# Key heads computed in spare weight columns and gathered by DMA, and value products taken in pairs, in a one-core attention and feed-forward kernel

## The chip, the cores and the metric

The kernel runs on one core of one Trainium2 chip. The metric is the device time of one execution in microseconds (us). Each kernel was run several times, on the same chip as the kernel that it is compared with and in the same rounds. The profiler's span of an execution is some 1.7 us shorter than its device time; times inside a profile count from the start of the span.

## The reference, cut to what matters

The sequence has 2048 positions of width 448. Sixteen heads of 28 columns attend to 8 keys, 2 positions apart. The attention output gates a feed-forward branch of width 1792.

```python
xn = layernorm(x)                                   # (1, 2048, 448)
qkv = (xn @ wqkv).reshape(B, S, 3, 16, 28)...       # q, k, v
idx = pos[:, None] - 2 * arange(8)[None, :]         # 8 keys, distance 2
logits = einsum("bhsd,bhswd->bhsw", q, k[idx]) * 28 ** -0.5   # masked where idx < 0
s = (softmax(logits) @ v[idx]) @ wo
g = silu(gelu(xn @ w1 + b1) @ w2 + b2)
return x + s * g
```

## The kernel before

Positions are split by parity, so that a distance of 2 becomes a distance of 1. There are four chunks of 512 positions and 17 attention units of 121 queries. A stage is the first feed-forward product of one chunk, then the q and k projections of the next chunk, then (in the first three stages) five attention units, each beside one tile of the second feed-forward product. I call the stages first, second and last by the five units that they hold (0 to 4, 5 to 9, 10 to 14). Within a stage I number the units from 0.

The 448 rows of contraction are three times 128 and a rest of 64. Two rests share the array: one uses its upper 64 rows, the other its lower 64 rows. I call such a product half-height. Heads lie four to a group, each in a slot of 32 columns of which 28 are the head's.

```python
    def qk_weights(which, kt):
        r = slice(0, P) if kt < 3 else slice(64 * which, 64 * which + 64)
        src = wraw[r, kt, D * which:D * which + 32]
        nc.vector.tensor_copy(wqk[r, kt, H * which:H * which + H, :],
                              bass.AP(src.tensor, src.offset, [list(src.ap[0]), [DH, H], [1, 32]]))

    def qk_full(c, g, ps, first, copies):          # six products, 128 rows of contraction
        for w in range(2):                         # w = 0: q, w = 1: k
            for kt in range(3):
                nc.tensor.matmul(ps[w][:, :], wqk[:, kt, 16 * w + 4 * g:16 * w + 4 * g + 4, :],
                                 xnT[:, kt, LEAD + c * CH:LEAD + (c + 1) * CH], ...)
            ...
    # qk_rest: the two half-height products; qk_pair(c, g): both, for head group g of chunk c

    def qk_put(c, g, w, ps, copies):
        copies[w]((qT, kT)[w][:, g, LEAD + c * CH:LEAD + (c + 1) * CH], ps[w][:, :])

    def v_mm(b):                                   # value product of block b: four products
        ps = psB.tile([P, D], F32, name="ps_v", tag="B")
        o = LEAD + QB * b - 7
        for kt in range(KT):
            nc.tensor.matmul(ps[:, :], xnT[:, kt, o:o + P], wv[:, kt, :], ...)
        return ps
    ...
        # one stage
        feed_forward_1(c, ps, ...)                 # holds qk_pair(c + 1, 0)
        qk_pair(n, 1, True, DD)                    # n = c + 1
        for i in range(5):
            b = next(units)
            if i == 0:
                E = qk_unit(b, lambda: qk_pair(n, 2, False, ...))   # scores S, exp, mask
                ...
                qk_pair(n, 3, True, DA)
            else:
                E = qk_unit(b)
                norm()
                ffn2_job(4 * c + i - 1)            # y
                v_job(next(vs))
                if n + 1 < NC:
                    ln_apply(4 * n + 3 + i)
                    ln_dma(4 * n + 3 + i)          # SyncE: transpose into xnT
            norm = av_unit(b, E)                   # O, attention times values
```

Nearly every transfer is issued from SyncE, in program order: the loads of weights and x at the start, `late_loads()` (the last 512 rows of x and 16 pieces of `wo`) after the first four transposes, the transposes of normalised x, and the stores of finished output tiles `o_t`, of which there are three buffers.

The softmax here doesn't subtract the row's maximum and nothing guards it: scores larger than these inputs give would overflow.

## Time and profile before

| | before |
|---|---|
| median of the first three runs | 167.68 us (167.32 to 167.9) |
| profiled span | 165.6 us |
| TensorE (PE) busy | 158.9 us, 96% |
| its longest wait after the start | under 0.4 us |

These are two lines of the timeline of SyncE's queue (start in us, length of the group in us, line, operation, destination and source, count).

```profile
27.30 8.16 SPq L140 DMA_DIRECT2D wo<-in_A_wo_dram  x16
...
41.65 13.69 SPq L184 DMA_TRANSPOSE xnT<-xnb  x4
```

The reader is to see that the queue issues one transfer after another, that sixteen small ones took 8.16 us of it, and that it was then free from 35.46 to 41.65, before the transposes that the second stage's projections need.

### The profile page before, as it was taken

The page shows a single profiled execution, that of the slowest core. Times are in us where ns is not written, and L with a number is a line of the kernel's source. Part 1 is how long each engine was busy: PE and PEld are TensorE (multiplying, and loading weights), DVE is VectorE, ACT ScalarE, POOL GpSimd, SP SyncE. Part 2 cuts the span into 40 slices and gives each one's busy share as a digit, 9 for nine tenths or more (in the row PEclk, how much of TensorE's full clock was granted, in tenths as well). Part 3 has the DMA queues.
Part 4 walks back from the last instruction along what each step waited for, and adds up shares of the span by engine and source line. Part 5 has one row for each costly group of instructions (what it writes and reads, how often), then busy time and mean ns, then how long its engine had stood idle before and what let it go on. Part 6 is the DMA issues. An engine that isn't in the chain of part 4 may idle for free.

```text
span 165.6 us, 3242 instructions
## 1 busy us (share of the span) xinstructions
PE 158.9 (96%) x1290; PEld 71.8 (43%) x1301; DVE 112.9 (68%) x256; ACT 125.9 (76%) x198; POOL 4.5 (3%) x16
## 2 busy tenths in 40 slices
PE   6899999999999999999999999999999999999990
PEld 2343333345554334445554334335555334445570
DVE  5967890497888638687888308877777507678893
ACT  3773698598887795998887795698888698698830
POOL 7002000000000000000000000000000000000000
PEclk9999999999999999999999999999999999999999
DMA  5999995520111100100211100300000002020011
GB/s 134 302 306 267 325 190 93 164 44 4 32 36 32 32 0 4 55 0 0 36 32 32 36 0 0 112 1 4 0 4 0 0 0 60 31 83 0 4 55 55
DMA packets 15963, 10.62 MB, mean 64 GB/s; under 512 B 7500, under 2 KB 15948, under 8 KB 15948
## 3 DMA queue, kind: packets, MB, share of 16 engines
q1 hardware_dynamic: 15660, 10.18, 24.0%
q10 hardware_dynamic: 288, 0.23, 0.5%
q8 instruction: 10, 0.16, 0.4%
q14 instruction: 5, 0.04, 0.1%
HBM read 7.00 MB, written 1.84 MB: 53 GB/s over the span
## 4 chain that ended last, share of the span: by engine, by line
PE 83%; ACT 7%; DVE 5%; DMA 2%; issue 1%; DVEq 0%
PE ps_y L281 23%; PE ps_h L249 21%; PE ps_qk L197 11%; PE ps_v L228 8%; PE ps_s L331 6%; PE ps_h L258 4%; PE S L355 3%; PE psO L370 3%; ACT hT L264 3%; PE ps_qk L207 3%; DMA x<-in_A_x_dram 2%; ACT th L310 1%; DVE sg L337 1%; DVE st L161 1%; ACT L509 1%
## 5 line engine op out<-in xcount | busy, mean ns | idle before, releaser
L264 ACT ACTIVATE hT<-ps_h,b1f 128x512 bf16<-128x512 f32 x56 | 34.1, 695 | 10.1 <-PE ps_h L258 7.3
L249 PE MATMUL ps_h<-xnT,w 128*128 128x512 bf16 x161 | 39.3, 380 | 0.5 <-issue 0.2
L281 PE MATMUL ps_y<-w,hT 128*128 128x448 bf16 x196 | 39.5, 353 | 0.0
L361 ACT ACTIVATE E<-S 128x976 bf16<-128x976 f32 x34 | 31.6, 983 | 2.1 <-PE S L355 0.8
L281 PEld LDWEIGHTS <-hT 128*128 128x128 bf16 x196 | 18.0, 98 | 16.7
L249 PEld LDWEIGHTS <-w 128*128 128x128 bf16 x168 | 15.0, 98 | 22.1 <-issue 6.4
L363 DVE TENSOR_TENSOR E<-E,mk_gen 128x976 bf16<-128x976 bf16 x30 | 20.0, 666 | 6.7 <-ACT E L361 6.5
L197 PE MATMUL ps_qk<-xnT,wqk 128*128 128x512 bf16 x92 | 22.2, 380 | 0.3 <-issue 0.2
L379 DVE TENSOR_TENSOR oT<-psO,den 128x484 bf16<-128x484 f32 (+1 forms) x17 | 11.3, 662 | 10.1 <-ACT den L378 10.1
L214 DVE CAST qT<-ps_qk 128x512 bf16<-128x512 f32 x16 | 11.0, 687 | 9.5 <-PE ps_qk L207 8.4
L228 PE MATMUL ps_v<-wv,xnT 128*128 128x448 bf16 x68 | 15.7, 353 | 0.1
L311 DVE SCALAR_TENSOR_TENSOR g<-th,y 128x448 bf16<-128x448 bf16 x13 | 7.6, 621 | 10.8 <-ACT th L310 10.8
L337 DVE SCALAR_TENSOR_TENSOR sg<-ps_s,g 128x448 bf16<-128x448 f32 (+2 forms) x17 | 10.1, 592 | 7.0 <-PE ps_s L331 6.9
L233 ACT CAST vw<-ps_v 128x448 bf16<-128x448 f32 x17 | 9.1, 533 | 6.9 <-PE ps_v L228 6.8
L197 PEld LDWEIGHTS <-wqk 128*128 128x128 bf16 x96 | 8.9, 98 | 11.5 <-issue 1.8
L331 PE MATMUL ps_s<-wo,oT 128*128 128x448 bf16 (+2 forms) x68 | 13.4, 342 | 0.0
L377 ACT ACTIVATE den<-den 128x484 f32<-128x484 f32 (+1 forms) x17 | 10.3, 605 | 4.0 <-DVE den L374 4.0
L374 DVE STREAM_SHUFFLE den<-psO 128x484 f32<-128x484 f32 (+1 forms) x17 | 11.7, 695 | 0.0
L378 ACT ACTIVATE den<-den 128x484 f32<-128x484 f32 (+1 forms) x17 | 10.3, 606 | 0.5
L161 DVE BATCH_NORM_STATS2 st<-x 128x6 f32<-128x448 bf16 x16 | 9.8, 610 | 0.9 <-DMA x<-in_A_x_dram 0.8
L331 PEld LDWEIGHTS <-oT 128*128 128x128 bf16 x68 | 6.4, 98 | 5.9 <-issue 0.2
L228 PEld LDWEIGHTS <-xnT 128*128 128x128 bf16 x68 | 6.3, 98 | 6.0 <-ACT xnT L181 0.6
(71 smaller groups left out, 139.8 us busy)
## 6 DMA issues: line engine op xcount, KB each, us to landing
out_dram<-o_t SPq DMA_DIRECT2D x15, 112.0 KB
w<-in_B_w_dram SPq DMA_DIRECT2D x1, 1568.0 KB
x<-in_A_x_dram SPq DMA_DIRECT2D x3, 448.0 KB
w<-in_B_w_dram SPq DMA_DIRECT2D x2, 672.0 KB
wraw<-in_A_wqkv_dram SPq DMA_DIRECT2D x1, 672.0 KB
w<-in_B_w_dram SPq DMA_DIRECT2D x4, 112.0 KB
wo<-in_A_wo_dram SPq DMA_DIRECT2D x16, 24.5 KB
wv<-in_A_wqkv_dram SPq DMA_DIRECT2D x1, 336.0 KB
```

The source lines that it names most:

```text
L161: nc.vector.bn_stats(out=st[:], in_=xt(t))
L197: nc.tensor.matmul(ps[w][:, :], wqk[:, kt, 16 * w + 4 * g:16 * w + 4 * g + 4, :], xnT[:, kt, LEAD + c * CH:LEAD + (c + 1) * CH], start=(fi ...
L228: nc.tensor.matmul(ps[:, :], xnT[:, kt, o:o + P], wv[:, kt, :], start=(kt == 0), stop=(kt == KT - 1))
L249: nc.tensor.matmul(ps[i][:, :], w1[:, kt, m * P:(m + 1) * P], xnT[:, kt, LEAD + c * CH:LEAD + (c + 1) * CH], start=(first and kt == 0), st ...
L264: nc.scalar.activation(hT[:, m, :], ps[i][:, :], ACT.Gelu_apprx_tanh, bias=b1f[:, m:m + 1])
L281: nc.tensor.matmul(ps[:, :], hT[:, m, tt * P:(tt + 1) * P], w2[:, m, :], start=(m == 0), stop=(m == MT - 1))
L331: nc.tensor.matmul(ps[:, 0:n], oT[:, g, t * P:(t + 1) * P], wo[:, g, cs], start=(g == 0), stop=(g == 3))
L337: nc.vector.scalar_tensor_tensor(out=sg[:, cs], in0=ps[:, 0:cs.stop - cs.start], scalar=0.5, in1=g_sb[t % NG][:, cs], op0=ALU.mult, op1=AL ...
L361: nc.scalar.activation(ev, Sp[p2][:, :, :, 0:QW], ACT.Exp, scale=SCALE)
L363: nc.vector.tensor_tensor(out=ev, in0=ev, in1=mkb, op=ALU.mult)
L374: nc.vector.stream_shuffle(den[:, :, 0:n], psO[:, :, 0:n], [0] * 32)
L379: nc.vector.tensor_tensor(out=oT[:, :, QB * b:QB * b + n], in0=psO[:, :, 0:n], in1=den[:, :, 0:n], op=ALU.mult)
```

## The change

The intent is to take products from PE. A slot of 32 columns has 4 that belong to no head, and PE computes them anyway. Sixteen q slots and the twelve k slots of groups 0 to 2 have 28 x 4 = 112 spare columns, just the 4 x 28 of the last four k heads. So `qk_spare` puts the weights of those heads there, the product for group 3 shrinks to q alone (`q3_job`), and small transfers gather the results, four rows each, into group 3 of `kT`: 28 a chunk, 84 in chunks 1 to 3. Chunk 0 keeps the old way. Secondly, the value products of two blocks share the array for their rests, like the projections. The order of half-height products, the output tiles and the loads is changed to suit.

```diff
+    def qk_spare(kt):
+        for r, s0, s1 in ((slice(0, P), 0, NS),) if kt < 3 else (...):
+            ...                        # NS = 28; four columns of a k head into columns 28 to 31 of a slot
+    def k3_rows(c, g, w):
+        j = 4 * w + g
+        cols = slice(LEAD + c * CH, LEAD + (c + 1) * CH)
+        for h in range(4):
+            nc.sync.dma_start(kT[32 * h + 4 * j:32 * h + 4 * j + 4, 3, cols],
+                              (qT, kT)[w][32 * h + DH:32 * h + 32, g, cols])
...
     def qk_put(c, g, w, ps, copies):
+        if isinstance(copies[w], list):
+            copies[w].append(lambda: qk_put(c, g, w, ps, DD))
+            return
         copies[w]((qT, kT)[w][:, g, LEAD + c * CH:LEAD + (c + 1) * CH], ps[w][:, :])
+        if c:
+            k3_rows(c, g, w)
...
+    def q3_job(c, copy):
+        ps = psB.tile([P, CH], F32, name="ps_qk", tag="B")
+        for kt in range(KT):
+            nc.tensor.matmul(ps[:, :], wqk[:, kt, 12:16, :], xnT[:, kt, ...], ...)
+        qk_put(c, 3, 0, [ps], [copy])
...
+    def v_pair(b):                     # six products of 128 rows, then two of 64 side by side
+        ps = [psB.tile([P, D], F32, name="ps_v", tag="B") for _ in range(2)]
+        ...
+        for i in range(2):
+            v_put(b + i, ps[i])
...
-        late_loads()
...
                 if i == 0:
-                    E = qk_unit(b, lambda: qk_pair(n, 2, False, (..., lambda *a: tail.append(a))))
+                    E = qk_unit(b, lambda: qk_pair(n, 2, False, (nc.vector.tensor_copy, late)))
                     ...
-                    qk_pair(n, 3, True, DA)
+                    late[0]()
+                    v_pair(4 * n)
+                    if c == 0:
+                        late_loads()
                 else:
                     ...
-                    v_job(next(vs))
+                    if i == 2:
+                        v_pair(4 * n + 2)
+                    if i == 4 and c == 2:
+                        v_job(16)
                     ...
+            ps = ffn1(n, 0, False)
             norm()
-            ps = ffn1(n, 0, True)
```

## The prediction

> **What bounds the kernel now.** I read the busy shares first, then the slices, the chain that ended last, and then the timeline of one stretch after another, because a share alone does not say whether TensorE (PE) waits.
>
> ```profile
> PE 158.9 (96%) x1290; PEld 71.8 (43%) x1301; DVE 112.9 (68%) x256; ACT 125.9 (76%) x198; POOL 4.5 (3%) x16
> ...
> PE   6899999999999999999999999999999999999990
> ...
> PE 83%; ACT 7%; DVE 5%; DMA 2%; issue 1%; DVEq 0%
> ```
>
> PE is busy in every slice after the first, and the chain is 83% PE. The timeline shows how fast it really runs. L249 is the first feed-forward product with all 128 rows, L258 its last 64 rows of contraction, where two products share the array.
>
> ```profile
> 19.20 0.60 PE L258 MATMUL ps_h<-xnT,w 64*128 64x512 bf16 x4
> 19.73 2.76 PE L249 MATMUL ps_h<-xnT,w 128*128 128x512 bf16 x12
> 22.43 0.61 PE L258 MATMUL ps_h<-xnT,w 64*128 64x512 bf16 x4
> ```
>
> Twelve products of 512 columns take 22.43 - 19.73 = 2.70 us and four half-height ones 0.53 us. With 0.216 us a slot of 512 columns (12 x 0.216 = 2.59; 2 x 0.216 = 0.43) each change between full and half height costs 0.10 to 0.11 us. Fourteen products of 448 columns (L281, below) take 2.66 us, 0.19 us each.
>
> The attention units (17 blocks of 121 queries) are the second thing to read. L355 is scores S, L281 the second feed-forward product y, L228 the value product, L370 attention times values (O).
>
> ```profile
> 40.62 0.39 PE L355 MATMUL S<-qT,kT 28*128 28x122 bf16 x16
> 40.95 2.82 PE L281 MATMUL ps_y<-w,hT 128*128 128x448 bf16 x14
> 41.05 1.86 ACT L361 ACTIVATE E<-S 128x976 bf16<-128x976 f32 x2
> 42.80 0.61 ACT L377 ACTIVATE den<-den 128x484 f32<-128x484 f32 x1
> 42.95 0.67 DVE L363 TENSOR_TENSOR E<-E,mk_gen 128x976 bf16<-128x976 bf16 x1 [0.16 <-ACT E L361]
> 43.44 0.61 ACT L378 ACTIVATE den<-den 128x484 f32<-128x484 f32 x1
> 43.61 0.92 PE L228 MATMUL ps_v<-wv,xnT 128*128 128x448 bf16 x4
> 44.08 0.66 DVE L379 TENSOR_TENSOR oT<-psO,den 128x484 bf16<-128x484 f32 x1 [0.46 <-ACT den L378]
> 44.46 0.40 PE L370 MATMUL psO<-E,vw 128*32 128x122 bf16 x16
> 44.56 0.54 ACT L233 CAST vw<-ps_v 128x448 bf16<-128x448 f32 x1 [0.52 <-PE ps_v L228]
> 44.79 0.40 PE L355 MATMUL S<-qT,kT 28*128 28x122 bf16 x16
> ```
>
> A unit takes 44.79 - 40.62 = 4.17 us. O needs the second masked exp, which ends at 42.95 + 0.67 = 43.62, 3.00 us after S began; PE gets to O only after 3.84 us. That slack of 0.84 us is almost exactly the value product between them (43.61 to 44.46, 0.85 us).
>
> PE does wait in the first units of chunks 2 and 3 (S 69.30 to 69.90 and O 73.24 to 73.78, where 0.33 us each is usual): 0.27 + 0.21 = 0.48 us, and the same again at 108.16 and 112.09, 0.96 us in all.
>
> ```profile
> 68.26 1.26 ACT L264 ACTIVATE hT<-ps_h,b1f 128x512 bf16<-128x512 f32 x2
> 69.30 0.67 PE L355 MATMUL S<-qT,kT 28*128 28x122 bf16 x16
> 69.54 1.28 ACT L412 ACT_TABLE_LOAD   x1
> 73.24 0.61 PE L370 MATMUL psO<-E,vw 128*32 128x122 bf16 x16
> ```
>
> The last gelu still holds the score buffer at 69.30, and the table load behind it delays exp.
>
> **What the Trainium skill says.** "TensorE: Matmul & The Clock Gate", section "Wait — 56ns, not 53.3ns?", gives 215.7 ns start to start for 512 columns once warm; the trace agrees (0.216 us). "TensorEngine Tiling (Array Packing)", Key Properties, says that changing the tiling mode drains the engine; the trace puts that at 0.10 to 0.11 us. "DMA: Bandwidth & Descriptors", Anatomy of one DMA, gives a fixed cost near 2 us on the GpSimd path; the first load of x here, issued from SyncE at 0.81, released VectorE at 3.63. "Perfetto Trace Analysis", Identifying Performance Opportunities, says that a repeated bubble can mean too few buffers; the score wait above is one.
>
> **The change part by part.**
> (1) Projections of chunks 1 to 3: a pair for head group 3 is 6 full products and one shared slot, 7 slots; the new q-only job is 4. Nine slots x 0.216 = 1.94 us less. The missing keys come out in columns that the other slots compute anyway.
> (2) Value products: six pairs, each 7 slots rather than 8: 6 x 0.19 = 1.14 us less.
> (3) Changes of array mode, counted in the instruction order of both kernels: 99 before, 101 after, +0.21 us. PE's own work is thus 1.94 + 1.14 - 0.21 = 2.87 us shorter, all on the path.
> (4) The q job and the output products now stand between the last gelus and S. In chunks 2 and 3 the score buffer is then free in time. From the last half-height gelu product to S there are 0.43 + 0.10 + 6 x 0.216 + 0.10 = 1.93 us, and gelu starts 0.42 us into them (as at 25.66 and 26.10); 1.27 + 1.28 us later, with 0.03 of hand-over, exp starts, at S + 1.07. The mask ends 2.57 us after that and the next S follows 0.37 us later (as after 73.40), at S + 4.01, where PE alone (0.33 + 0.32 + 1.30 + 1.53 of products and 0.33 for O) would be at S + 3.81: a wait of 0.20 us. Of the 0.96 us of waits 0.40 us remain.
> (5) Units lose their slack. Units 1, 3 and (chunks 1 and 2) 4 have no value product: PE reaches O at S + 0.33 + 2.66 + 0.10 = 3.09 us, against 3.00 us for exp and mask. Two value copies on ScalarE after a pair push the next exp to about O + 0.97 us (0.13 + 2 x 0.42, the pitch my estimate) instead of O + 0.76: then 0.97 + 2.57 + 0.37 - 0.33 - 3.42 = 0.16 us of stall, four times (units 1 and 3 of the first chunk, unit 3 of the others), 0.64 us.
> (6) VectorE falls behind in unit 4 of the first two chunks, where normalised x is still made beside the unit. From exp of unit 3 the chain is 3.03 (second exp, Ln and Exp of the unit before) + 1.63 (oT, y, normalise: 0.58 + 0.53 + 0.52) + 0.59 (shuffle) + 0.58 (mask 1) + 0.67 (mask 2) + 0.37 = 6.87 us, durations from the timeline; PE's own order needs 6.36. Stall 0.51 us. The next feed-forward product now begins with both half-height products, and the second needs the buffer that oT of unit 3 frees, some 0.54 us later still. Twice 1.05 = 2.10 us.
> (7) 84 small transfers from SBUF to SBUF gather the keys, 28 a chunk. The 16 wo loads in the old kernel issue at a median of 0.383 us. The first unit that reads the gathered keys is unit 4, 3 and 2 of the three stages. In the last, 16 transfers must issue after the second pair's copies: 0.3 + 16 x 0.38 = 6.4 us, with 1.6 to 2 us to land, 8.0 to 8.4 us after the first S, where the need is at about 7.9. I put 0.3 us there; the other two stages have over 3 us to spare.
> (8) At the start two memsets go and two larger ones come on VectorE, inside the 0.84 us that it waits for x; the extra 168 KB of loads (three of 56 KB) follow what the start needs. Nothing.
> Sum: 167.68 - 2.87 - 0.96 + 0.40 + 0.64 + 2.10 + 0.30 = 167.29 us.
>
> **The rivals.**
> A: the waits of (5) and (6) don't come, because exp and mask run a little ahead of my chain. For it: my stalls are differences of 0.1 to 0.5 us between long sums, and the change reorders work around just these places. Against: before, VectorE idles only 0.46 + 0.16 us in a unit of 4.17 us, and the unit shrinks to 3.4. Time: 167.68 - 2.87 - 0.56 = 164.3 to 165 us.
> B: the gather is the new bound. For it: all transfers go through one queue, in order, among output stores. Against: only the last stage is tight. With 0.45 us an issue and 2 us to land, 0.3 + 7.2 + 2 - 7.9 = 1.6 us of stall: 168.6 us.
> C: the copies moved from ScalarE to VectorE (0.69 us a chunk) make it the bound of the whole stage. Against: its feed-forward stage has idle stretches of up to 5.9 us. It would add under 1 us.
>
> **Range and chances.** The working says 167.3; A pulls down by up to 2.7 and B up by 1.4, and A seems the likelier, so I choose 166.9, with 165.0 to 169.0 as the range. Over 2% faster is below 164.3: every wait would have to vanish, 0.09. Over 2% slower is above 171.0: only B far beyond its estimate, 0.04. Within 2%: 0.87.
>
> **What would show it.** Steps 1 to 3: full-height projection products 90 in the program rather than 96, and between waits PE's stretches shorter by 0.65 us a projection and 0.19 us a value pair. Step 4: S of chunks 2 and 3 taking 0.33 us. Steps 5 and 6: O of units 1, 3 and 4 at 0.5 us or more in place of 0.40, with the mask named as releaser, and a gap at the first half-height product after unit 4. Step 7: a DMA releasing S in unit 2 of the last stage. The prediction is wrong if units without a value product take 3.4 us each with no gap (A), or if a gap of over 1 us stands before S (B).

## The result and the profile after

| | before | after |
|---|---|---|
| median of 4 runs | 167.72 us (167.32 to 167.9) | 182.58 us (181.59 to 184.64) |
| profiled span | 165.6 us | 180.6 us |

The changed kernel took 1.087 times the time of the kernel before (95% interval 1.0818 to 1.0922). All ratios here are the mean time of one kernel's fast runs over the mean time of the other's fast runs in the same rounds, so they are not quite the ratios of the medians. Executions over 1.5% slower than the fastest of the same kernel are left out of the means. One run of the changed kernel, 184.64 us, counts as slow and is left out of the ratio. The time is 13.6 us above the top of the predicted range.

The page of the changed kernel answers to the lines of the prediction (busy shares, PE in 40 slices, granted clock in 40 slices, the chain that ended last).

```profile
PE 162.5 (90%) x1278; PEld 72.4 (40%) x1289; DVE 114.9 (64%) x261; ACT 122.7 (68%) x192; POOL 4.5 (3%) x16
...
PE   7999998999999499999998999758299999999991
...
PEclk9999999999999969999999999999659999999998
...
PE 48%; DVE 22%; ACT 15%; DMA 7%; issue 3%; SPq 2%; DVEq 0%
```

PE now has two holes, a small one in slice 14 (59 to 63 us) and a large one in slices 26 to 29 (113 to 131 us). The granted clock drops behind both of them. PE carries only 48% of the chain, and SyncE's queue (SPq) appears in it, with the line of the gather. PE is also busy for longer with fewer instructions: 1278 are the 12 fewer that the change removes, but some of them ran at a lower clock.

The timeline of SyncE's queue after the change says what happened there (same columns as before).

```profile
30.39 2.63 SPq L209 DMA_DIRECT2D kT<-qT  x4
...
45.83 2.44 SPq L209 DMA_DIRECT2D kT<-kT  x4
48.31 0.44 SPq L139 DMA_DIRECT2D x<-in_A_x_dram  x1
48.80 8.06 SPq L143 DMA_DIRECT2D wo<-in_A_wo_dram  x16
56.96 5.16 SPq L187 DMA_TRANSPOSE xnT<-xnb  x4
...
107.17 2.49 SPq L209 DMA_DIRECT2D kT<-qT  x4
...
114.84 2.97 SPq L383 DMA_DIRECT2D out_dram<-o_t  x4
...
126.81 2.44 SPq L209 DMA_DIRECT2D kT<-kT  x4
```

The first chunk's gather keeps the queue from 30.39 to 48.27, 17.9 us without a break. Behind it stand the loads of `wo`, and behind those the transposes, which begin at 56.96 where they began at 41.65 before. In the last stage the gather and four output stores issue from 107.17 to 129.25. The row of the gather's line in the view by source line (duration of one issue in ns, smallest, median, largest) shows why.

```profile
L209 SPq DMA_DIRECT2D kT<-qT x48: 577/577/707, 30.4 to 126.1; - x48
```

One issue takes SyncE 577 ns. The four of a group, at 2.44 us from the first start to the last end, stand 0.62 us apart; 28 of them, with the small gaps between groups, are the 17.9 us above. The loads of `wo`, from which the prediction borrowed its 0.383 us, still take 0.383 us in this kernel.

Three things then wait for the queue. First, the projection of the second stage waits for the transposes. These are two lines of PE's timeline (the bracket names what ended a wait and how long it was).

```profile
63.65 0.61 PE L225 MATMUL ps_qk<-xnT,wqk 64*128 64x512 bf16 x2 [3.09 <-DMA xnT<-xnb]
64.19 2.69 PE L215 MATMUL ps_qk<-xnT,wqk 128*128 128x512 bf16 x6
```

This group of six takes 2.69 us here, and 1.47 us at the same place in the version without the gather (below). Secondly, in the last stage VectorE waits for a free output buffer, because the stores stand in the queue behind the gather, and the copies that PE needs stand behind VectorE's wait. The first line is from VectorE's timeline.

```profile
117.06 0.39 DVE L382 TENSOR_TENSOR o_t<-x,sg 128x448 bf16<-128x448 bf16 x1 [4.45 <-DMA out_dram<-o_t]
```

```profile
119.17 1.33 PE L274 MATMUL ps_v<-wv,xnT 128*128 128x448 bf16 x6 [2.56 <-DVE qT L235]
```

Thirdly, unit 2 of the last stage waits for the gathered keys. Twelve of its 16 score products use groups 0 to 2 or keys that have landed; the last four each wait for a transfer. The last transfer was issued at 128.7 us and the last score product started at 130.51, so most of the delay is the issue, not the way of the data.

```profile
125.25 0.34 PE L397 MATMUL S<-qT,kT 28*128 28x122 bf16 x12
128.58 0.28 PE L397 MATMUL S<-qT,kT 28*128 28x122 bf16 x1 [2.98 <-DMA kT<-kT]
...
130.70 4.91 PE L325 MATMUL ps_y<-w,hT 128*128 128x448 bf16 x14
```

The scores took 5.45 us instead of 0.33. Behind them the 14 products of y took 4.75 us (to the next start, 135.45), where the prediction works out 2.66. The view of two stretches with their granted clock (length, busy time of PE, weight loads, VectorE, ScalarE and GpSimd, clock, share of DMA, GB/s) explains that, for this place and for the one behind the transposes.

```profile
63.60:66.70 3.10, 3.05 (x8) 1.03 (x9) 1.61 (x3) 0.19 (x1) 0.00 (x0) 0.50 0.00 0
130.60:135.50 4.90, 4.90 (x16) 2.00 (x16) 1.91 (x3) 2.08 (x3) 0.00 (x0) 0.55 0.00 0
```

The mean clock was 0.50 and 0.55. The Trainium skill, "TensorE: Matmul & The Clock Gate", Part 1, says that about 3.4 us without activity throttle PE to half rate, and that it takes about as long again at work to recover. The trace agrees on the half rate but not on the time before it. PE's last product before the keys ended at 125.59 us by the trace; the mean granted clock was 1.00 from 127 to 128, 0.65 from 128.0 to 128.5 and 0.50 from 128.5 to 129. So it fell at about 128.15 (an estimate from these means), 2.6 us into the wait. In the wait for the transposes the same working gives 2.7 us, and in the run with the loads first (below) 1.8 us. The idle stretch of 2.6 us in front of the value products at 119.17 was not followed by a drop: the clock was 1.00 from 119 to 121. It is a page that the prediction used for another number, and whose consequence it missed.

I compared starts on PE with its undisturbed pace (0.2158 us for 512 columns, 0.19 us for 448, 0.107 us for a change of array mode). That gives this account of the 15.0 us of span. The first line is a count times the pace, the second a wait measured in the kernel before, the last the remainder; the others are gaps beyond the pace.

| where | us |
|---|---|
| products and mode changes, steps 1 to 3 | -2.87 |
| score waits of the kernel before, step 4 | -0.96 |
| waits in units, steps 4 to 6 | +2.52 |
| transposes late (0.71 at 27.2, 3.26 at 60.4) | +3.97 |
| lower clock behind them | +1.46 |
| last stage: value products wait for copies behind stores | +2.88 |
| gathered keys (0.24, 0.27, 5.12) | +5.63 |
| lower clock behind the last of them | +2.09 |
| start of the program | -0.34 |
| not assigned, small | +0.6 |

The five lines that no step of the prediction has, or has only as 0.30 us, sum to 16.03 us. Not all of that is the gather's: the wait of 0.71 us at 27.2 comes before its first issue, at 30.39, and at this place the later runs, too, wait for between 0 and 0.5 us. It counts as scatter of the first transposes, and the earlier start makes up for half of it.

### The profile page after: what moved, and what is told of

Read it like the earlier page. It is cut to its first block, busy times and chain, and to the rows that moved or that the text cites. A ratio compares the mean times of both kernels' runs of the same rounds, so it can differ in the third digit from the quotient of the medians.

```text
span 180.6 us, 3339 instructions
## 1 busy us (share of the span) xinstructions
PE 162.5 (90%) x1278; PEld 72.4 (40%) x1289; DVE 114.9 (64%) x261; ACT 122.7 (68%) x192; POOL 4.5 (3%) x16
## 4 chain that ended last, share of the span: by engine, by line
PE 48%; DVE 22%; ACT 15%; DMA 7%; issue 3%; SPq 2%; DVEq 0%
PE ps_y L325 15%; PE ps_h L293 8%; PE ps_qk L215 7%; DVE st L164 4%; PE ps_s L373 3%; PE ps_v L274 3%; ACT den L420 3%; ACT E L403 3%; DMA xnT<-xnb 3%; ACT den L419 3%; ACT hT L308 3%; DVE den L416 2%; SPq L209 2%; PE S L397 2%; DVE sg L379 2%
## 5 line engine op out<-in xcount | busy, mean ns | idle before, releaser
L325 PE MATMUL ps_y<-w,hT 128*128 128x448 bf16 x196 | 41.6, 366 | 0.0
L325 PEld LDWEIGHTS <-hT 128*128 128x128 bf16 x196 | 18.6, 101 | 18.2 <-issue 2.5
L405 DVE TENSOR_TENSOR E<-E,mk_gen 128x976 bf16<-128x976 bf16 x30 | 19.4, 664 | 10.1 <-ACT E L403 10.1
L215 PE MATMUL ps_qk<-xnT,wqk 128*128 128x512 bf16 x74 | 19.2, 399 | 1.0 <-DMA xnT<-xnb 0.5
L263 ACT CAST vw<-ps_v 128x448 bf16<-128x448 f32 x17 | 8.5, 536 | 11.7 <-PE ps_v L278 10.5
L397 PE MATMUL S<-qT,kT 28*128 28x122 bf16 x272 | 8.2, 216 | 4.1 <-DMA kT<-kT 4.1
L215 PEld LDWEIGHTS <-wqk 128*128 128x128 bf16 x78 | 7.0, 101 | 11.4 <-issue 5.3
L302 PE MATMUL ps_h<-xnT,w 64*128 64x512 bf16 x56 | 10.3, 382 | 0.3 <-DVE oT L421 0.2
L274 PE MATMUL ps_v<-wv,xnT 128*128 128x448 bf16 x36 | 7.8, 352 | 2.6 <-DVE qT L235 2.6
L348 DVE TENSOR_TENSOR y<-ps_y,b2bc 128x448 f32<-128x448 f32 x14 | 8.6, 616 | 2.2 <-PE ps_y L325 2.2
```

Of the source, the lines that this page charges most:

```text
L274: nc.tensor.matmul(ps[i][:, :], xnT[:, kt, o:o + P], wv[:, kt, :], start=(kt == 0), stop=False)
L325: nc.tensor.matmul(ps[:, :], hT[:, m, tt * P:(tt + 1) * P], w2[:, m, :], start=(m == 0), stop=(m == MT - 1))
L405: nc.vector.tensor_tensor(out=ev, in0=ev, in1=mkb, op=ALU.mult)
```

## The experiments

My theory, Q in the expectations below, was that in-order issue on SyncE, at 0.58 us a transfer, is the whole cause, through the keys and through everything that stands behind them. One rival was that the keys' lateness alone matters, another that the reordered units (steps 5 and 6) cost more than I had worked out, and a third that only the loads and transposes in the queue matter. All times below are medians. The output of every experiment passed the comparison with the reference.

### The change without the gather

```diff
+    nc.gpsimd.memset(kT[:, 3, LEAD + CH:LEAD + S].bitcast(U32), 0)
...
-        if c:
-            k3_rows(c, g, w)
```

> The changed kernel without its 84 gather transfers; the keys of head group 3 in chunks 1 to 3 stay zero, so the output is wrong on purpose, while every product, copy and order on the four compute engines stays. Theory Q (the SyncE queue: 84 issues of 0.61 us hold back the transposes, the output stores and the keys, and each long wait of TensorE also lowers its clock): the 3.1 us wait for the transposes, the 2.6 us for the blocked copies, the 4.1 us for the keys and the slow clock after two of them all go; about 166.5 us (165.5 to 167.5), granted clock near 1.00. Rival U (the units and the new order of products cost it): 172 us or more, because nothing of that changes.

Measured: 167.07 us (166.77 to 167.21) beside 167.49; ratio 0.9971 (0.9941 to 1.0). The last four key heads of chunks 1 to 3 are zero here, so the result is wrong. The comparison nevertheless passed it, so for this input it cannot notice whether those keys are there; a pass says nothing about the gather in the runs below either.

The gather thus accounts for 1.087 - 0.997 = 0.090 of the time, some 15 us, and all the rest of the change together for no more than half a per cent (0.9971, and the interval reaches 1.0). The lines of PE's timeline show the waits that steps 5 and 6 had worked out (O of unit 3, O of unit 4, then the first half-height product).

```profile
48.65 0.57 PE L411 MATMUL psO<-E,vw 128*32 128x122 bf16 x16
...
52.74 0.39 PE L411 MATMUL psO<-E,vw 128*32 128x122 bf16 x14 [0.28 <-DVE E L404]
53.06 0.92 PE L301 MATMUL ps_h<-xnT,w 64*128 64x512 bf16 x2
```

By stage the waits beyond the pace are 1.37, 1.41 and 0.71 us, 3.49 in all. The sum 167.49 - 2.87 - 0.96 + 3.49 = 167.15 us meets the measured 167.07.

### The gather from GpSimd's queue

```diff
-            nc.sync.dma_start(kT[32 * h + 4 * j:32 * h + 4 * j + 4, 3, cols],
+            nc.gpsimd.dma_start(kT[32 * h + 4 * j:32 * h + 4 * j + 4, 3, cols],
```

> The changed kernel with the same 84 transfers issued from GpSimd's queue instead of SyncE's; the output stays right. Theory Q: SyncE's queue is as free as before the change, 166.5 to 168.5 us if GpSimd issues a transfer within about 0.9 us (28 in the 25 us between first copy and need). Rival L (the transfers themselves, 4 KB in 4 pieces, land too late, from whatever queue): a wait of 3 us or more for the gathered keys stays in the last stage, 172 us or more.

Measured: 170.69 us (169.2 to 170.76); ratio 1.0168 (1.012 to 1.0215), between the two expectations and in neither. An issue takes GpSimd 518 ns. The transfers landed 1.6 us after their issue at the least, 1.8 at the median and 3.6 at most. Nothing else uses that queue, so transposes, loads and stores are on time again, and 12 of the 15 us are gone. Beyond the version without the gather 3.3 us are left (1.0168 - 0.9971, of 167.5). The profiled execution is the fastest of the four, 169.2 us, with a span 2.2 us longer than without the gather, and one wait is about as long: the scores of unit 2 in the last stage took 2.52 us instead of 0.33. This is the first of its four waits for a key.

```profile
117.72 0.22 PE L397 MATMUL S<-qT,kT 28*128 28x122 bf16 x1 [0.55 <-DMA kT<-kT]
```

The other three executions, which have no profile, took some 1.5 us more at mean clocks of 0.986 to 0.99 against 1.0; a drop of the clock behind this wait would fit, but that isn't shown. So the keys alone are late by 2.2 us there even without anything else in their queue, which speaks against the rival that says they are the whole cause.

### The loads ahead of the gather

```diff
         nc.sync.dma_start(b2bc[:], ...)
+        late_loads()
...
-                    if c == 0:
-                        late_loads()
```

> The changed kernel with the loads of the last x chunk and of wo issued ahead of the first gather, as the kernel before had them, instead of behind it. Theory Q: the queue is as long as before, only the order differs. The transposes are in time, but the first gather starts some 5 us later and ends near 53 us, where unit 4 needs its keys at 49.6: a wait of 3.5 to 5 us moves there, 179 to 184 us. Rival M (moving these loads behind the gather was the fault): the wait for the transposes and its slow clock go and nothing takes their place, 4.5 us less or better, under 178.5 us.

Measured: 185.53 us (184.15 to 186.68); ratio 1.1071 (1.1007 to 1.1136). The transposes no longer wait, as expected, but the time rose, 1.5 us beyond the range that my theory gave. The queue's time is the same, and now the first stage's keys are behind the loads. PE's timeline in unit 4 of the first stage:

```profile
52.73 0.28 PE L397 MATMUL S<-qT,kT 28*128 28x122 bf16 x1 [3.33 <-DMA kT<-kT]
...
55.34 4.13 PE L325 MATMUL ps_y<-w,hT 128*128 128x448 bf16 x14
```

The scores there took 6.29 us, 5.96 more than usual, and the y behind them ran at a lower clock, 4.06 us from start to start instead of 2.75. Moving the loads only chooses who waits. The rival that blamed their place is out.

### The paired value products alone, on the kernel before

```diff
-                    v_job(next(vs))
+                    if i in (2, 4):
+                        v_pair(4 * n + i - 2)
```

> The kernel before with the shared rest of the value products alone: value pairs in units 2 and 4 of each stage in place of one product in units 1 to 4, projections as before, no gather. My steps 2, 3 and 5: 6 x 0.19 = 1.14 us of products less, 12 mode changes more or less cancelled (at most 0.6 us more), stalls of 0.1 to 0.5 us in units 1 and 3; 167.0 to 168.3 us. If the value pairs were the cause of the loss: above 171 us.

Measured: 168.73 us (168.56 to 169.5); ratio 1.0081 (1.0049 to 1.0113). Six pairs take 1.14 us of products from PE, but add six mode changes, an estimated 6 x 0.107 = 0.64 us; the kernel became 1.3 us slower, 0.4 us beyond the expected range. O of the same unit waits for ScalarE's copy of the pair, twice for 0.62 us in the last stage, besides 0.17 us in unit 3 of the first two stages. So the value pairs aren't the cause of the loss of 15 us. More doesn't follow for the change: this version has the pairs in units 2 and 4 and the change has them in units 0 and 2. In the last stage O needs the values of its own block, which are made just before it here and earlier in the change, and the run without the gather has no such wait. The units that lost their value product did get shorter: unit 1 of the first stage takes 3.41 us instead of 4.17.

### Two queues for the gather

```diff
-            nc.sync.dma_start(kT[...], ...)
+            (nc.sync, nc.gpsimd)[h // 2].dma_start(kT[...], ...)
```

> The changed kernel with the gather shared by two queues: heads 0 and 1 from SyncE, heads 2 and 3 from GpSimd, 14 transfers a chunk each. Theory Q: 14 x 0.61 = 8.5 us of SyncE and 14 x 0.51 = 7.1 us of GpSimd a chunk; the last stage's keys land some 1 us before or after unit 2 needs them (after the last copy only four transfers a pair of queues are left), the transposes and stores are in time: 166.7 to 168.0 us, as without any gather (167.07). Rival L (the transfers themselves are slow whatever the queue): 170 us or more, as from GpSimd alone (170.69).

Measured: 167.44 us (167.19 to 167.71) beside 167.14; ratio 1.0017 (1.0001 to 1.0034). Fourteen issues a chunk on each queue fit. That settles the theory: with the same 84 transfers, the same bytes and the same order of work on PE, nothing but who issues them takes some 14 us away (1.087 - 1.0017, of 167.5). The first line, from SyncE's queue, is that of the second stage's transposes, 10.15 us earlier than in the changed kernel; the second, from PE, the scores of unit 2 in the last stage, with no transfer named.

```profile
46.81 8.74 SPq L187 DMA_TRANSPOSE xnT<-xnb  x4
...
116.70 0.97 PE L397 MATMUL S<-qT,kT 28*128 28x122 bf16 x16
```

The Trainium skill, "DMA: Bandwidth & Descriptors", section "Issuing engines are not separate DMA queues", says that several issuing engines save only the time that a sequencer needs to issue, "which is usually small relative to the DMA itself". The first half agrees; the second doesn't in this case, where 28 issues of 0.58 us in a row are the cost.

No key was late here, yet the scores of units 4, 3 and 2 of the three stages took 0.51, 0.51 and 0.57 us longer than the usual 0.33.

### The same transfers in the kernel before, with nobody to wait for them

Here the kernel before issues 84 transfers of the same form from the same places into a tile that nothing reads.

```diff
+        if c and not (w == 1 and g >= 2):
+            dummies(c, g, w)
+    def dummies(c, g, w):
+        ...
+            nc.sync.dma_start(dum[32 * h + 4 * j:32 * h + 4 * j + 4, :],
+                              (qT, kT)[w][32 * h + DH:32 * h + 32, g, cols])
```

> The kernel before with 84 transfers of the same shape added to SyncE's queue at the same places, into a tile that nobody reads; the output stays right and no product moves. Theory Q: nobody waits for these keys, but the queue's other users are held back: the transposes of chunk 2 come some 1 us late, the fourth output store of a group of four delays VectorE by 2 to 3 us; 168.5 to 172 us. Rival K (only waiting for the gathered keys costs, not the queue): 167.3 to 168.0 us.

Measured: 169.4 us (168.95 to 169.69); ratio 1.0128 (1.0104 to 1.0152). The waits of VectorE and PE are those of theory Q in small: 0.88 us for the transposes at 60.6 us (another of 0.51, at 27.7, comes before the first added transfer and isn't theirs), and one for an output buffer (line, what it waited for, us in total, times, longest).

```profile
DVE o_t L350 <- DMA out_dram<-o_t: 3.0, 1, 3.0
```

So merely standing in the queue costs some 2 us (0.0128 of 167.1, less perhaps the 0.51) in the order of the kernel before, where the loads come ahead of the transfers and nothing needs their data. In the changed kernel late keys, and transposes behind the loads, come on top.

### What an issue costs, by shape

In one run the kernel before also issued groups of four transfers from SBUF to SBUF, of one shape each, in the last stage.

```diff
+        for r in range(4):
+            nc.sync.dma_start(dum[0:4, :], kT[0:4, 0, LEAD:LEAD + CH])
+        ...                            # 8, 16, 32, 64, 128 rows; 4 rows of 64 bytes; rows 28 to 31; 28 rows
```

> The kernel before with groups of four SBUF to SBUF transfers of 1 KB rows on SyncE at the end of the third stage, of 4, 8, 16, 32, 64, 128 rows, then 4 rows of 64 bytes, 4 rows from row 28, and 28 rows, to read the issue time of each shape. If issue time goes by rows, 4 rows are the shortest (I had taken 0.38 us from 28 rows of wo); if the number of DMA engines that take part sets it, few rows take longer: 4 rows near 0.58 us, 16 and more rows 0.33 to 0.4 us, and 64 bytes a row no less than 1 KB a row.

The single run (state unknown, 196.94 us) has no meaning as a time, because the repeated writes to one tile wait for each other. Its issue times do. The median issue on SyncE took 604 ns for 4 rows, 624 for 8, 516 for 16, 507 for 32, 477 for 64 and 468 for 128. With 64 bytes a row instead of 1024, four rows took 613; rows 28 to 31, as in the gather, 585; and 28 rows 749.

```profile
L386 SPq DMA_DIRECT2D dum<-kT x4: 577/604/717, 106.9 to 112.6; - x4
L396 SPq DMA_DIRECT2D dum<-kT x4: 465/468/486, 145.5 to 151.5; - x4
```

The first line is 4 rows and the second 128. I had expected 0.33 to 0.4 us from 16 rows on, and that was a miss. The issue time differs by shape, 64 bytes a row did not shorten it, and fewer rows are no cheaper. Why 4 and 28 rows cost more than 128 stays open. Whether one transfer could serve all four heads of a slot, 7 issues a chunk instead of 28, wasn't run.

### The order of the units, with two queues

This takes two queues and puts the work back where steps 4 to 6 saw waits: the first products with all rows ahead of the half-height ones, the normalisation of unit 3 moved to unit 2, and the q job and output products after the last first-feed-forward product.

```diff
-            if c < 3 and k == (6 if c == 0 else 5):
+            if c < 3 and k == 6:
                 q3_job(c + 1, nc.vector.tensor_copy)
...
-                        ln_apply(4 * n + 3 + i)
-                        ln_dma(4 * n + 3 + i)
+                        for t in {1: (4,), 2: (5, 6), 3: (), 4: (7,)}[i]:
+                            ln_apply(4 * n + t)
+                            ln_dma(4 * n + t)
...
-            ps = ffn1(n, 0, False)
+            ps = ffn1(n, 0, True)
```

> The split gather, and three edits for the stalls of my steps 4 to 6: the feed-forward product after unit 4 begins with its full-height products again, unit 3 makes no normalised x (unit 2 makes two), and the q job and the output products stand after the last gelu's products in chunks 2 and 3. If steps 4 to 6 name the right waits, the 0.54 + 0.50 us at the end of the first two stages, the 0.34 us at the end of the third and 0.2 us in two first units go, 2.8 us in all, and some six stalls of 0.17 us stay: 164.0 to 165.5 us. If these stalls are from something else (ScalarE's total, say) they stay: 166.5 us or more.

Measured: 166.81 us (166.43 to 167.16); ratio 0.9979 (0.9958 to 0.9999), a miss by over 1 us. The waits that it aimed at did go, but for 0.13 us behind unit 4 of the second stage, and a new one of 0.40 us, for gelu, came at 101.5 us. And the scores of the three units that first read gathered keys took 0.99, 0.81 and 0.85 us, with no transfer named in a wait. PE's timeline for unit 4 of the first stage, then the row of the score line's semaphore instructions on the queue of weight loads, in the view by source line:

```profile
48.99 0.44 PE L397 MATMUL S<-qT,kT 28*128 28x122 bf16 x14
49.61 0.44 PE L397 MATMUL S<-qT,kT 28*128 28x122 bf16 x2 [0.18 <-issue]
```

```profile
L397 PEldq EVENT_SEMAPHORE  x24: 51/51/51, 48.8 to 116.7; - x24
```

PE works through instructions that wait for the gathered pieces, in front of the score products, even where the waits are satisfied: 24 extra instructions of 51 ns, eight a unit, are 0.41 us of the 0.48 to 0.66 us. The run without the gather has none of them.

### One early wait for all keys

This moves those waits to a place where PE has other products to run. A product of one column that loads the gathered keys as its weights stands ahead of O in the unit before; its result is overwritten. The version is that of the section before, and also zeroes the gathered rows of `kT` at the start.

```diff
-    def av_unit(b, E):
+    def av_unit(b, E, keys=0):
         psO = psB.tile([P, 4, P], F32, name="psO", tag="B")
+        if keys:
+            k0 = LEAD + keys * CH
+            nc.tensor.matmul(psO[:, 0, 0:1], kT[:, 3, k0:k0 + P], wz[:, 0:1], start=True, stop=True)
```

> The reordered kernel with split gather, and one product of a single column ahead of O in units 3, 2 and 1 of the three stages that loads all the gathered keys once, so that the score products of the next unit no longer carry the 16 waits on the transfers. In the reordered kernel S of units 4, 3 and 2 takes 0.99, 0.81 and 0.85 us instead of 0.33, with 24 wait instructions of 51 ns on TensorE's weight queue, although the transfers landed before. Theory W (satisfied waits cost TensorE their instruction time where products are only 12 ns apart): S is 0.33 us again, the waits disappear behind the y products, 1.0 to 1.7 us less than 166.8: 165.1 to 165.9 us. Rival D (the keys really come late there): no gain, O of the unit before waits instead, 166.5 us or more.

Measured: 166.43 us (166.13 to 167.03); ratio 0.9946 (0.9925 to 0.9966), half of what was expected. The scores are back at 0.33 us:

```profile
48.98 0.40 PE L398 MATMUL S<-qT,kT 28*128 28x122 bf16 x16
```

In the first two stages, then, the waits in front of the scores were the cost. In the last one the early product itself waited 0.9 us: the keys really were not there yet (the wait of its weight load, 1.28 us, ends with a key's transfer). Besides, the first-feed-forward products waited 0.4 us for gelu in each of two stages.

### Half of the value copies on VectorE

```diff
-            v_put(b + i, ps[i])
+            (nc.scalar.copy, nc.vector.tensor_copy)[i](
+                vw[:, b + i, :, 1:DH + 1], ps[i][:, :].rearrange("p (h c) -> p h c", h=H))
```

> The same, and the second value copy of each pair on VectorE instead of ScalarE. If my step 5 is right (two copies in a row on ScalarE push exp of the next unit by 0.2 us, six stalls of 0.17 to 0.18 us), O of units 1 and 3 takes 0.33 us and the time falls by another 1.0 us: 164.1 to 165.0 us. If exp is set by something else, or VectorE then is late with the mask, no change or slower.

Measured: 166.52 us (166.13 to 167.56); ratio 0.9952 (0.9927 to 0.9977). 164.1 to 165.0 us had been expected. Three of the four waits of 0.17 us at O went, so step 5 had the mechanism right: it is ScalarE's two copies that delay exp. But two other waits at O grew by 0.14 us each (at 48.70 and 85.55 us), the first transposes came 0.3 us late, and no time was gained.

### The q job earlier, alone and with those copies

Two last versions start from the one with the early wait. They put the q job between the first-feed-forward products 4 and 5 in the second and last stage, so that gelu has more time before the next half-height products, and leave out the early wait in the last stage. The second of them also has the copies on VectorE.

```diff
-            if c < 3 and k == 6:
+            if c < 3 and k == (6 if c == 0 else 4):
                 q3_job(c + 1, nc.vector.tensor_copy)
...
-                norm = av_unit(b, E, n if i == 3 - c else 0)
+                norm = av_unit(b, E, n if c < 2 and i == 3 - c else 0)
```

> The fence kernel with two edits: in chunks 2 and 3 the q job stands between the fourth and fifth feed-forward pair, which gives the gelus 0.86 us more before the next half-height products (they waited 0.41 and 0.40 us), and the last stage has no early load of the keys (it waited 0.93 us before O there, where waiting at S cost 0.52 us). If these readings are right 0.8 to 1.2 us less than 166.43: 165.2 to 165.7 us. If ScalarE's total sets this stretch, the wait moves to the next products: no change.

> The same with the second value copy of each pair on VectorE. In the earlier pair this took away three of four stalls of 0.17 us at O and gave no time. If that was the scatter of one transpose that came 0.3 us late at the start, this is 0.3 to 0.6 us faster than the kernel beside it; if VectorE gives it back, the same.

Measured: 165.46 us (165.36 to 165.59) beside 167.63, ratio 0.9877 (0.9855 to 0.9898); and with the copies 165.15 us (164.93 to 165.56), ratio 0.9862 (0.9836 to 0.9887). Both beat the kernel before, by 1.2 and 1.4%, and the changed one; between the two the intervals overlap. In the profile of the faster the span is 163.4 us and PE is busy for 156.4 us of it, 96% as in the kernel before: 2.5 us less of work, and 0.0138 x 167.5 = 2.3 us less of time. Unit 2 of the last stage still takes 0.53 us more for its scores, for the waits in front of them.

## Why the prediction was right and wrong

- **Steps 1 to 3, PE's own work: right.** PE has 12 instructions fewer, as nine slots of projections less mean (three times a pair of 8 became a job of 4), and the run without the gather closes with these terms to within 0.1 us.
- **Step 4: right.** The score waits of 0.96 us are gone; O of the first unit of the second and last stage lost 0.20 us each in the run without the gather, as worked out.
- **Step 5: right.** Units 1 and 3 of the first stage and unit 3 of the others lost 0.17 or 0.18 us each in that run, against 0.16.
- **Step 6: right.** Unit 4 with the half-height product behind it lost 1.03 us in each of the first two stages without the gather, against 1.05. The last stage lost 0.34 us at the same product, which no step had. All told 3.49 us against 3.14.
- **Step 7: wrong, and it is the error.** It took "a median of 0.383 us" from the loads of `wo`, which go from DRAM to SBUF, for an issue from SBUF to SBUF. That issue took 0.577 us, and 0.62 us from one to the next within a group. It then asked only whether the keys come in time: "the other two stages have over 3 us to spare". It never asked what stands behind 28 issues in an in-order queue. Behind them stood, in turn, loads, transposes and output stores. The term was 0.30 us; the runs put 15 us in its place (1.087 with the gather against 0.997 without), of which the two-queue run gives back some 14. The prediction's own sign for B, a gap of over 1 us before S, came: 2.98 us.
- **No step for the clock.** Behind the late transposes and the late keys PE ran at a lower clock, 1.46 + 2.09 = 3.55 us of the loss.
- **Step 8: right.** Without the gather the projection of the next chunk began at 27.53 us, against 27.51 before. (In the changed kernel PE was 0.34 us early at first and 0.35 late at this place, the scatter named above.)
- **Rivals.** A did not happen: the waits came. C did not either: VectorE was busy for 64% of the span, and the sum without the gather closes without such a term. B named the cause, but its estimate of 1.6 us kept the borrowed kind of issue (0.45 us) and counted one wait in one stage. The range followed from B, so it was far too narrow.

What stays open: why an issue of four rows takes 0.58 us and one of 28 rows 0.75, the remainder of the score delay beyond the counted semaphore instructions, and the 0.34 us in the last stage of the run without the gather.

## What to carry to other kernels

Before adding small transfers to a queue, multiply their number by the issue time of a transfer of that very kind, and then go through everything that stands behind them in that queue, not only through those who read their data. A long wait on TensorE must be charged again for the slow clock after it: here the waits of 3.1 and 3.0 us for transposes and keys brought 1.46 and 2.09 us more, and one of 2.6 us nothing. And when several small products are joined, look at who waits for the copies behind them: in the version with value pairs alone, two waits of 0.62 us ate the gain.

## What the Trainium skill lacked or had wrong

- "DMA: Bandwidth & Descriptors", Anatomy of one DMA, lists about 50 ns of dispatch on the GpSimd path, and the page has no issue time measured by the shape of a small transfer within SBUF (only a vendor's cycle count per instruction for earlier generations, without a shape). The runs show 518 ns of GpSimd's queue, and on SyncE 577 ns for four rows in the gather and 468 to 749 ns over the shapes tried, no less with 64 bytes a row than with 1024.
- The same page, "Issuing engines are not separate DMA queues", calls the issue time usually small. For small transfers in a row it was the whole cost: 17.9 us for the first chunk's 28 on one queue, and 1.087 against 1.0017 of the time for one queue against two.
- No page that I read gives the cost of waits that are already satisfied in front of TensorE's products: 51 ns for each semaphore instruction, and scores of 0.81 to 0.99 us instead of 0.33. ("Advanced Engine Details and Errata" has a time only for a sequencer's reading of a semaphore.)
- "TensorEngine Tiling (Array Packing)", Key Properties, names the drain at a change of tiling mode without a figure: 0.10 to 0.11 us here.
- "TensorE: Matmul & The Clock Gate", Part 1, puts the throttle after an idle window of about 3.4 us. Here the clock was halved about 2.6 and 2.7 us into the waits for keys and transposes and in one run 1.8 us (estimates from the mean clocks of short stretches), and the slow stretches cost 2.09 and 1.46 us.
